# Hash attention with a gated FFN: keys' signs masked for either head on ScalarE, key operands scaled by a power of two, queries' signs spread by a transfer

## The chip, the cores and the metric

The kernel runs on one core of a Trainium2 chip. The metric is the device time in microseconds (us) of one execution. Beside it stands one execution that the hardware profiler recorded; all trace times below come from it, counted from the start of its span.

## What is computed

Four batches of eight heads, 768 positions, head dimension 64. Every query and every key gets six sign bits from a projection; a query attends only to keys whose six bits are all equal to its own. The attention output, as 3072 tokens by 512, goes through a gated FFN with 1536 hidden units.

```python
q_bits = (np.einsum('bhsd,dk->bhsk', q, proj) > 0)       # k_bits alike
mask = q_bucket[:, :, :, None] == k_bucket[:, :, None, :]
scores = np.where(mask, (1/8) * q @ k.T, -1e9)
attn = softmax(scores) @ v                                # per head
x = attn.transpose(0, 2, 1, 3).reshape(3072, 512)
out = (silu(x @ w_gate) * (x @ w_val)) @ w_out
```

## The kernel before

**Units.** Two heads form a pair, and there are 16 pairs, four to a batch (`NP` = 4). Each pair has two halves of 384 queries, and each half six key chunks (`NCH`) of 128 keys. `score(u)` (lines 451 to 464) makes one chunk's scores for both heads: float32 products of `kT` and `qT`, then bfloat16 products of the sign rows `kb` and `qb` added into the same bank (both are line 461), then an exponential on ScalarE (line 464) into `weights(u)`, called `room` or `A` in the trace. `add` (489, 493) sums the exponentials on VectorE. After six chunks `attend` (475) multiplies them with `vraw`, and ScalarE copies the result to `xT` (482).

**Signs.** `front(n)` prepares pair n. For the first five pairs (`n <= NP`, here called the early pairs) TensorE transposes q and k (378), and ScalarE copies them out (381); for later pairs VectorE transposes (423). Four products with `hash_w` (391) put the projections of two query halves and two key halves into four blocks of 32 partitions of one bank, `hps`. In each block partitions 0 to 15 belong to the first head and 16 to 31 to the second. Four ScalarE instructions take the signs (397) into the low 32 rows of `qb` and `kb`. Then `spread` writes the second set of rows, 64 to 95: for `kb` two VectorE multiplications by a column (406), one for either head, with zeros for the other head's rows; for `qb` a VectorE copy (409) in pairs 0 to 4, and a transfer on SP's queue (411) in later pairs. The columns `nudge` and `times_k` are built at the start (141 to 156). The sum of the sign products is zero for a matching key and at most minus 2**35 else, since `times_k` carries 2**34.

**The order.** The program's order is written out by hand, and each engine works through its own instructions in it. Up to pair 3 the main loop (735 to 778) does for each half: six times `score` and `add`; attention; then a number of steps of weight preparation (`prepare_on`, from `narrow`, 293 to 298, and `form`, 327, on VectorE; `scale_to`, 279 and 280, on ScalarE). In the second half of pair n the hash of pair n+1 comes after the sixth chunk, with its four signs at once, and `spread` is put on the list `rest`, which `finish(rest)` empties after the attention, ahead of the preparation. In the first half of a pair, `total(n-1)` comes after the second chunk: it sums the accumulators with products (506), takes the reciprocal on VectorE (514) and sends it over the partitions by eight transfers on SP's queue (519); `norm` then scales `xT` on VectorE (526). The bank of these sums is the same one that attention uses in the first batch.

**Loads.** `load(n+2)` stands at the end of pair n and puts q, k and v on SP's queue. q and k have one buffer each, v has two.

**Later.** From pair 4 on (`LATE`), products of the FFN (`up`, `po`, line 550) fill TensorE between the halves, and `chores`, one after each product step, hold the signs and `spread` of the next pair. The first `up` products need `xT` of the first two pairs, the second block those of pairs 2 and 3.

Of the kernel before, what the change touches and what calls it, by code (L numbers as in the profile page):

```python
# [8 lines left out]
FP32 = mybir.dt.float32  # L9
# [3 lines left out]
ALU = mybir.AluOpType  # L13
AF = mybir.ActivationFunctionType
AX = mybir.AxisListType
# [3 lines left out]
def kernel(  # L19
# [57 lines left out]
    def fetch(n, name, queue, half=None):  # L77
        b, pr = pairs[n]
        if name == "v":
            t = raws["v", n] = raw.tile([P, 2, NCH, D], FP32, tag="vraw", name="vraw")  # L80
            queue.dma_start(
                t.rearrange("p h c d -> p h (c d)"),
                v[b, 2 * pr : 2 * pr + 2].rearrange("h (p c) d -> p h (c d)", c=NCH),
            )
            return
        src = q if name == "q" else k
        if not half:
            raws[name, n] = raw.tile([P, NCH, 2, D], FP32, tag=name + "raw", name=name + "raw",
                                     bufs=1)
        t = raws[name, n]  # L90
        if n <= NP:
            cs = slice(None) if half is None else slice(half * CH, (half + 1) * CH)
            for h in range(2):
                queue.dma_start(t[:, cs, h, :],
                                src[b, 2 * pr + h].rearrange("(p c) d -> p c d", c=NCH)[:, cs, :])
            return


        blocks = t.rearrange("p c a b -> p (c a b)").rearrange(
            "p (c a d) -> p c a d", a=P // BLOCK, d=BLOCK)  # L100
        for h in range(2):
            for x in range(D // BLOCK):
                at = h * D + x * BLOCK
                queue.dma_start(
                    blocks[at : at + BLOCK],
                    src[b, 2 * pr + h][:, x * BLOCK : (x + 1) * BLOCK].rearrange(
                        "(a p c) d -> p c a d", c=NCH, p=BLOCK))

    def load(n):
        for name in "qkv":  # L110
            fetch(n, name, nc.sync)

    two_proj = konst.tile([P, NBITS], FP32, tag="proj", name="proj")
    for o in (0, D):
# [23 lines left out]


    HR = 16  # L140
    assert NBITS + 1 <= HR and 2 * HR == BLOCK
    rules = wraw.tile([P, PIECE, 2], I32, tag="words", name="rules").rearrange("p f w -> p (f w)")
    rules = rules.bitcast(FP32)[:, 0 : 3 * P].rearrange("p (x r) -> p x r", r=P)

    nc.gpsimd.memset(rules[:, 0, :], -(2.0**-120))
    nc.gpsimd.memset(rules[:, 1:3, :], 0.0)
    groups = rules.rearrange("p x (g r) -> p x g r", r=HR)
    nc.gpsimd.memset(groups[:, 0, :, NBITS : NBITS + 1], 1.0)
    for h in range(2):
        g = groups[:, 1 + h, h, :]  # L150
        nc.gpsimd.memset(g[:, 0:NBITS], OFF / 2)
        nc.gpsimd.memset(g[:, NBITS : NBITS + 1], -NBITS * OFF / 2)
    nc.vector.tensor_tensor(rules, rules, ident.unsqueeze(1).to_broadcast([P, 3, P]), op=ALU.mult)
    columns = konst.tile([P, 3], FP32, tag="columns", name="columns")
    nc.vector.tensor_reduce(out=columns, in_=rules, axis=AX.X, op=ALU.add)
    nudge, *times_k = (columns[0:BLOCK, x : x + 1] for x in range(3))

    hash_w = konst.tile([P, BLOCK], FP32, tag="hash", name="hash")
    nc.vector.memset(hash_w, 0.0)
# [210 lines left out]
    def front(n):  # L370


        def transpose(name, half):
            if (name, n) not in T:
                T[name, n] = opnd.tile([P, S], FP32, tag=name + "T", name=name + "T")
            ps = bank("tps")
            for i in range(CH):
                nc.tensor.transpose(ps[:, i * P : (i + 1) * P],
                                    raws[name, n][:, half * CH + i, :, :].rearrange("p h d -> p (h d)"),
                                    ident)  # L380
            nc.scalar.copy(T[name, n][:, half * HQ : (half + 1) * HQ], ps[:, 0:HQ])

        bits["q", n] = sides["q", n % 2]
        bits["k", n] = sides["k", n % 2]

        def hash_blocks(todo, own):


            tile_ = bank("hps")
            for i, (name, half) in enumerate(todo):  # L390
                nc.tensor.matmul(tile_[i * BLOCK : (i + 1) * BLOCK, 0:HQ], hash_w,  # L391
                                 T[name, n][:, half * HQ : (half + 1) * HQ],
                                 start=True, stop=True)
            low, high = slice(0, BLOCK), slice(D, D + BLOCK)

            def sign(i, name, half):
                nc.scalar.activation(bits[name, n][low, half * HQ : (half + 1) * HQ],
                                     tile_[i * BLOCK : (i + 1) * BLOCK, 0:HQ], AF.Sign, bias=nudge)

            def spread():  # L400
                for name in sorted({name for name, _ in todo}):
                    hs = [half for x, half in todo if x == name]
                    b = bits[name, n][:, hs[0] * HQ : (hs[-1] + 1) * HQ]
                    if name == "k":
                        for to, times in ((high, times_k[1]), (low, times_k[0])):
                            nc.vector.tensor_scalar(b[to], b[low], scalar1=times, scalar2=None,  # L406
                                                    op0=ALU.mult)
                    elif own:
                        nc.vector.tensor_copy(b[high], b[low])
                    else:  # L410
                        nc.sync.dma_start(b[high], b[low])

            return [lambda i=i, at=at: sign(i, *at) for i, at in enumerate(todo)] + [spread]

        def hash_at_once(todo):
            *signs, spread = hash_blocks(todo, True)
            for f in signs:
                f()
            return [spread]

        def transpose_blocks(name):
            T[name, n] = opnd.tile([P, S], FP32, tag=name + "T", name=name + "T")
            nc.vector.transpose(T[name, n], raws[name, n].rearrange("p c h d -> p (c h d)"))

        order = [("q", 0), ("q", 1), ("k", 0), ("k", 1)]
        if n > NP:

            return ([lambda name=name: transpose_blocks(name) for name in "qk"]
                    + [lambda: hash_blocks(order, False)])
        turns = [lambda x=x: transpose(*x) for x in order]  # L430
        if n == 0:
            return [turns[2], turns[0], lambda: hash_at_once([("k", 0)]),
                    lambda: hash_at_once([("q", 0)]), turns[3], turns[1],
                    lambda: hash_at_once([("k", 1), ("q", 1)])]
        return turns[2:] + turns[:2] + [lambda: hash_at_once(order)]


    units = [(n, half, c) for n in range(len(pairs)) for half in range(2) for c in range(NCH)]
# [9 lines left out]
    def weights(u):  # L448
        return ((early_ring if u < MOVE else late_ring) + ring)[u % NCH]

    def score(u):
        n, half, c = units[u]
        qs = slice(half * HQ, (half + 1) * HQ)
        ks = slice(c * P, (c + 1) * P)
        sc = [bank("sc")[:, 0:HQ] for _ in range(2)]
        for x, start in ((T, True), (bits, False)):
            if u < 2 and not start:
                prepare_pair(1)
            for h in range(2):
                rows = slice(h * D, (h + 1) * D)  # L460
                nc.tensor.matmul(sc[h], x["k", n][rows, ks], x["q", n][rows, qs],  # L461
                                 start=start, stop=not start)
        for h in range(2):
            nc.scalar.activation(weights(u)[:, h, 0:HQ], sc[h], AF.Exp, scale=SCALE)  # L464

    def attend(u):
        n, half, c = units[u]
# [259 lines left out]
    def finish(todo):  # L727
        while todo:
            todo.pop(0)()
# [5 lines left out]
    for u in range(0, N, NCH):  # L735
# [5 lines left out]
                nc.gpsimd.memset(t[:, :, HQ:AW], 1.0)  # L741
        for c in range(NCH):
            score(u + c)
            if u + c == 2 or not gating and half == 1 and c == NCH - 1:
                prepare_pair(1)
                if u == 0:
                    finish(rest)
            if c == 1 and half == 0 and 0 < n <= NP:
                total(n - 1)
            if c:  # L750
                add(u + c)
        if n <= NP:
            finish(waiting)
        if not gating and half == 0:
            steps = front(n + 1)
        if not gating and half == 0 and u > 0:
# [4 lines left out]
            attend(u + c)  # L761
        if not gating:
            scale_ahead()
        if half == 1 and n + 2 < len(pairs):
            load(n + 2)
        if not gating and half == 0:
            prepare_pair(2 if u > 0 else 4)
        finish(first)
        finish(rest)
        prepare_on(0 if u == LATE else 4)  # L770
        chores = []
        if half == 1 and n >= NP:
# [67 lines left out]
```

The softmax here doesn't subtract the row's maximum and nothing guards it: scores larger than these inputs give would overflow.

## Time and profile before

| what | value |
|---|---|
| three runs | median 1007.13 us (1006.35 to 1008.91) |
| profiled execution, its own time | 1007.6 us |
| its span | 1005.8 us |
| TensorE (PE) busy | 991.4 us, 99% |
| VectorE (DVE) busy | 577.2 us |
| ScalarE (ACT) busy | 392.3 us |
| scores `sc`, float32 and bfloat16 parts | 162.3 us and 66.2 us |
| FFN `up` products | 260.9 us and 197.4 us |
| granted TensorE clock, mean | 0.997 |

The profile gives each engine's busy time, the waits (who waited for whom, in total us, number of times and the longest), the chain of work that ended last, and a timeline of every engine. Busy shares are averages over stages with different limits; the stage of the early pairs lies between about 8 and 119 us, and the rest of the span is the late stage. A name in a row stands for a buffer, with the line of the program beside it.

### The profile page before, as it was taken

To read this page: it belongs to the slowest core of one execution; us is meant where nothing else is said; L and a number is where in the kernel's file an instruction comes from. 1 tells how busy PE (TensorE), PEld (TensorE's weight loads), DVE (VectorE), ACT (ScalarE), POOL (GpSimd) and SP (SyncE) were. 2 spreads that over 40 slices of the span, in tenths; PEclk is the share of its full clock that TensorE was granted. 3 is DMA by queue.
4 is the path that set the end of the run, shared out by engine and by line. 5 is a ranking of instruction groups with operands and counts; after the bars stand their busy time and mean duration, and the time that the engine had idled before them with its cause. 6 is when DMAs were issued, how large, how long until landed. Compare 5 with 4: busy or idle time off the path is not lost.

```text
span 1005.8 us, 12454 instructions
## 1 busy us (share of the span) xinstructions
PE 991.4 (99%) x4597; PEld 600.8 (60%) x4597; DVE 577.2 (57%) x904; ACT 392.3 (39%) x877; POOL 101.0 (10%) x195
## 2 busy tenths in 40 slices
PE   9988899999999999999999999999999999999998
PEld 4444455555566775555557776555555787555687
DVE  5888898888884615556454543545556442435431
ACT  6877456555433214334341223334443211222200
POOL 3222132231000000000000000000000000111000
PEclk9999999999999999999999999999999999999999
DMA  7776586876313032423430304242122011323001
GB/s 228 215 243 215 157 214 186 230 241 180 103 37 84 24 76 83 105 91 90 105 107 23 75 20 116 76 104 83 56 85 80 22 37 63 104 77 115 29 28 36
DMA packets 120557, 106.75 MB, mean 106 GB/s; under 512 B 89200, under 2 KB 103888, under 8 KB 120496
## 3 DMA queue, kind: packets, MB, share of 16 engines
q0 software_dynamic: 19104, 73.28, 22.8%
q1 hardware_dynamic: 100592, 32.48, 14.1%
q8 instruction: 36, 0.59, 0.2%
q10 hardware_dynamic: 800, 0.20, 0.1%
q14 instruction: 25, 0.20, 0.1%
HBM read 81.79 MB, written 17.30 MB: 99 GB/s over the span
## 4 chain that ended last, share of the span: by engine, by line
PE 89%; DVE 6%; DMA 1%; SPq 1%; issue 1%; ACT 1%; DVEq 0%; POOL 0%
PE up L550 43%; PE po L550 21%; PE sc L461 12%; PE av L475 10%; DVE acc L493 1%; SPq L519 1%; PE sum L506 1%; PE hps L391 1%; DMA words<-in_moe_w_out_dram 1%; DVE wo L514 1%; DVE room L295 1%; DVE room L327 1%; DMA wo<-wo 1%; DVE room L293 0%; PE idle L134 0%
## 5 line engine op out<-in xcount | busy, mean ns | idle before, releaser
L550 PE MATMUL up<-xT,room 128*128 128x384 f32 x768 | 260.9, 488 | 0.0
L550 PEld LDWEIGHTS up<-xT,room 128*128 128x128 f32 x768 | 144.6, 190 | 106.7 <-issue 9.8
L550 PE MATMUL up<-xc,room 128*128 128x384 f32 x576 | 197.4, 486 | 0.0
L461 PE MATMUL sc<-qT,kT 64*128 64x384 f32 x768 | 162.3, 498 | 0.5 <-DVE c L537 0.5
L550 PEld LDWEIGHTS up<-xc,room 128*128 128x128 f32 x576 | 109.4, 190 | 76.3
L493 DVE TENSOR_TENSOR acc<-acc,A 128x768 f32<-128x768 f32 x128 | 122.7, 958 | 15.4 <-ACT A L464 1.8
L309 POOL DMA_DIRECT2D room<-ram x96 | 51.9, 541 | 714.7 <-PE up L550 707.6
L554 DVE TENSOR_TENSOR c<-c,up 128x384 f32<-128x384 f32 x72 | 39.9, 554 | 138.3 <-PE up L550 137.9
L464 ACT ACTIVATE A<-sc 128x384 f32<-128x384 f32 x256 | 105.4, 504 | 7.5 <-PE sc L461 7.5
L461 PEld LDWEIGHTS sc<-qT,kT 64*128 64x128 f32 x768 | 68.7, 189 | 53.8 <-issue 46.8
L685 ACT COPY o<-po 128x256 f32<-128x256 f32 x48 | 17.9, 372 | 200.5 <-PE po L550 200.5
L475 PE MATMUL av<-A,vraw 128*64 128x384 f32 (+1 forms) x512 | 88.2, 486 | 0.0
L536 ACT ACTIVATE th<-c 128x384 f32<-128x384 f32 x72 | 37.6, 523 | 127.5 <-DVE c L537 88.8
L461 PE MATMUL sc<-qb,kb 64*128 64x384 bf16 x384 | 66.2, 325 | 8.4 <-DVE kb L406 8.4
L554 DVE TENSOR_TENSOR o<-o,po 128x256 f32<-128x256 f32 x36 | 15.2, 421 | 99.0 <-PE po L550 70.0
L464 ACT ACTIVATE room<-sc 128x384 f32<-128x384 f32 x128 | 54.2, 496 | 40.8 <-PE sc L461 40.8
L550 PE MATMUL po<-wo,hid 128*128 128x256 f32 x288 | 66.9, 382 | 0.0
L550 PE MATMUL po<-wo,room 128*128 128x256 f32 x288 | 66.3, 379 | 0.1
L550 PE MATMUL po<-room,hid 128*128 128x256 f32 x288 | 66.1, 379 | 0.0
L475 PEld LDWEIGHTS av<-A,vraw 128*64 128x64 f32 x512 | 36.7, 137 | 46.1 <-issue 45.2
L613 ACT COPY c<-up 128x384 f32<-128x384 f32 x72 | 34.4, 478 | 69.7 <-PE up L550 69.7
L550 PEld LDWEIGHTS po<-wo,hid 128*128 128x128 f32 x288 | 54.1, 190 | 12.1 <-issue 4.9
(107 smaller groups left out, 967.8 us busy)
## 6 DMA issues: line engine op xcount, KB each, us to landing
room<-ram POOLq DMA_DIRECT2D x48, 512.0 KB, 4.7
room<-ram POOLq DMA_DIRECT2D x48, 384.0 KB, 3.9
vraw<-in_v_dram SPq DMA_DIRECT2D x16, 384.0 KB, 3.2
ram<-room POOLq DMA_DIRECT2D x12, 512.0 KB, 5.0
out_dram<-o SPq DMA_DIRECT2D x48, 128.0 KB, 1.7
room<-in_moe_w_out_dram POOLq DMA_DIRECT2D x10, 512.0 KB, 6.3
qraw<-in_q_dram SPq DMA_DIRECT2D x48, 96.0 KB, 3.2
hid<-in_moe_w_gate_dram POOLq DMA_DIRECT2D x9, 512.0 KB, 6.8
```

Of the source, the lines that this page charges most:

```text
L295: nc.vector.scalar_tensor_tensor(out=wi, in0=hi, scalar=-(1 << 31), in1=wi, op0=ALU.bitwise_and, op1=ALU.bitwise_or)
L309: nc.gpsimd.dma_start(places[k % 2][:, PARTS[go], :], ram[k % NG][:, PARTS[go], :])
L327: nc.vector.tensor_tensor(o, x, y, op=op)
L461: nc.tensor.matmul(sc[h], x["k", n][rows, ks], x["q", n][rows, qs], start=start, stop=not start)
L464: nc.scalar.activation(weights(u)[:, h, 0:HQ], sc[h], AF.Exp, scale=SCALE)
L475: nc.tensor.matmul(ps[h * D : (h + 1) * D, 0:width], raws["v", n][:, h, c, :], a[:, h, 0:width], start=c == 0, stop=c == NCH - 1)
L493: nc.vector.tensor_tensor(acc[n, half], acc[n, half], a[:, :, 0:HQ], op=ALU.add)
L536: nc.scalar.activation(th, g, AF.Tanh, scale=0.5)
L550: nc.tensor.matmul(ps, a, x, start=start and i == 0, stop=i == len(pairs_) - 1, skip_group_check=True)
L554: nc.vector.tensor_tensor(o, a, b, op=op)
L613: nc.scalar.copy(tile_of(g, spot), c)
L685: nc.scalar.copy(o, c)
```

## The change

The sign rows change for all pairs. Keys now carry a constant row for each bit that makes the sum zero on a match: rows 0 to 5 of a head's group are signs, rows 6 to 11 are constant, +1 for queries and -1 for keys. There are eight columns of constants instead of three, on 32 partitions.

For the early pairs the transposed key is copied out multiplied by 2**-34, the sign products are small whole numbers, and the exponential's scale has the factor 2**34. Pairs 1 to 4 take the key signs straight from the bank in four ScalarE instructions, one for each half and head, with a column as scale and another as bias, so that the other head's rows become zero; the two VectorE multiplications and the query copy are gone. The query rows are spread by a transfer on SP's queue. Pair 0 keeps the VectorE steps, with columns of ones and zeros.

The hash of the next early pair moves from after the sixth chunk to after the fourth; its two query signs and their transfer follow at once, and its key signs are put on `rest`, which is now emptied between the last score and the attention. For pairs 0 to 3 the loads of q and k of pair n+2 are issued at the end of the first half of pair n instead of the second; v stays. In the late pairs the transfer of the query rows and the multiplications of the key rows become two chores, in this order, instead of one.

```diff
+    def load(n, names):
+        if n < len(pairs):
+            for name in names:
+                fetch(n, name, nc.sync)
...
+    NUDGE = -(2.0**-120)
+    nc.gpsimd.memset(rules[:, 2:8, :], 0.0)
+    nc.gpsimd.memset(rules[:, 0:2, :], NUDGE)
     groups = rules.rearrange("p x (g r) -> p x g r", r=HR)
+    nc.gpsimd.memset(groups[:, 0, :, NBITS : 2 * NBITS], 1.0)
+    nc.gpsimd.memset(groups[:, 1, :, NBITS : 2 * NBITS], -1.0)
     for h in range(2):
+        nc.gpsimd.memset(groups[:, 2 + h, h, 0:NBITS], NUDGE)
+        nc.gpsimd.memset(groups[:, 2 + h, h, NBITS : 2 * NBITS], -1.0)
+        nc.gpsimd.memset(groups[:, 4 + h, h, 0 : 2 * NBITS], 1.0)
+        nc.gpsimd.memset(groups[:, 6 + h, h, 0 : 2 * NBITS], OFF / 2)
...
+    nudge = {"q": columns[0], "k": columns[1]}
+    one_head = columns[2:4]
+    mask, times_k = columns[4:6], columns[6:8]
...
-            nc.scalar.copy(T[name, n][:, half * HQ : (half + 1) * HQ], ps[:, 0:HQ])
+            nc.scalar.activation(T[name, n][:, half * HQ : (half + 1) * HQ], ps[:, 0:HQ], AF.Copy,
+                                 scale=2 / OFF if name == "k" else 1.0)
...
+            def sign(i, name, half, to=low, **how):
+                nc.scalar.activation(bits[name, n][to, half * HQ : (half + 1) * HQ],
+                                     tile_[i * BLOCK : (i + 1) * BLOCK, 0:HQ], AF.Sign,
+                                     **(how or {"bias": nudge[name]}))
+
+            return [lambda i=i, at=at, **how: sign(i, *at, **how) for i, at in enumerate(todo)]
+
+        def spread_k(times, cols=slice(0, S)):
+            b = bits["k", n][:, cols]
+            for to, by in ((high, times[1]), (low, times[0])):
+                nc.vector.tensor_scalar(b[to], b[low], scalar1=by, scalar2=None, op0=ALU.mult)
+
+        def spread_q():
+            nc.sync.dma_start(bits["q", n][high], bits["q", n][low])
+
+        def hash_own(*todo):
+            for f in hash_blocks(todo):
                 f()
+            for name, half in todo:
+                cols = slice(half * HQ, (half + 1) * HQ)
+                if name == "k":
+                    spread_k(mask, cols)
+                else:
+                    nc.vector.tensor_copy(bits["q", n][high, cols], bits["q", n][low, cols])
+
+        def hash_early(todo):
+            q0, q1, *ks = hash_blocks(todo)
+            q0()
+            q1()
+            spread_q()
+            return [lambda k=k, h=h: k(to=(low, high)[h], bias=one_head[h], scale=mask[h])
+                    for k in ks for h in range(2)]
+
+        def hash_late(todo):
+            return hash_blocks(todo) + [spread_q, lambda: spread_k(times_k)]
...
-            nc.scalar.activation(weights(u)[:, h, 0:HQ], sc[h], AF.Exp, scale=SCALE)
+            nc.scalar.activation(weights(u)[:, h, 0:HQ], sc[h], AF.Exp,
+                                 scale=SCALE * (OFF / 2 if n <= NP else 1.0))
...
-            if u + c == 2 or not gating and half == 1 and c == NCH - 1:
+            if u + c == 2 or not gating and half == 1 and c == NCH - 3:
                 prepare_pair(1)
-                if u == 0:
-                    finish(rest)
...
         if n <= NP:
             finish(waiting)
+            finish(rest)
...
-        if half == 1 and n + 2 < len(pairs):
-            load(n + 2)
-        if not gating and half == 0:
+        if half == 1:
+            load(n + 2, "qkv" if gating else "v")
+        elif not gating:
             prepare_pair(2 if u > 0 else 4)
+            load(n + 2, "qk")
         finish(first)
-        finish(rest)
```

More of the change, by code (lines that the diff above doesn't have):

```diff
@@ L107, in fetch @@
                         "(a p c) d -> p c a d", c=NCH, p=BLOCK))
-    def load(n):
-        for name in "qkv":
-            fetch(n, name, nc.sync)
+    def load(n, names):
+        if n < len(pairs):
+            for name in names:
+                fetch(n, name, nc.sync)
     two_proj = konst.tile([P, NBITS], FP32, tag="proj", name="proj")
@@ L140 @@
     HR = 16
-    assert NBITS + 1 <= HR and 2 * HR == BLOCK
+    assert 2 * NBITS <= HR and 2 * HR == BLOCK
     rules = wraw.tile([P, PIECE, 2], I32, tag="words", name="rules").rearrange("p f w -> p (f w)")
-    rules = rules.bitcast(FP32)[:, 0 : 3 * P].rearrange("p (x r) -> p x r", r=P)
-    nc.gpsimd.memset(rules[:, 0, :], -(2.0**-120))
-    nc.gpsimd.memset(rules[:, 1:3, :], 0.0)
+    rules = rules.bitcast(FP32)[0:BLOCK, 0 : 8 * BLOCK].rearrange("p (x r) -> p x r", r=BLOCK)
+    NUDGE = -(2.0**-120)
+    nc.gpsimd.memset(rules[:, 2:8, :], 0.0)
+    nc.gpsimd.memset(rules[:, 0:2, :], NUDGE)
     groups = rules.rearrange("p x (g r) -> p x g r", r=HR)
-    nc.gpsimd.memset(groups[:, 0, :, NBITS : NBITS + 1], 1.0)
+    nc.gpsimd.memset(groups[:, 0, :, NBITS : 2 * NBITS], 1.0)
+    nc.gpsimd.memset(groups[:, 1, :, NBITS : 2 * NBITS], -1.0)
     for h in range(2):
[L150 to L156, printed above, removed]
+        nc.gpsimd.memset(groups[:, 2 + h, h, 0:NBITS], NUDGE)
+        nc.gpsimd.memset(groups[:, 2 + h, h, NBITS : 2 * NBITS], -1.0)
+        nc.gpsimd.memset(groups[:, 4 + h, h, 0 : 2 * NBITS], 1.0)
+        nc.gpsimd.memset(groups[:, 6 + h, h, 0 : 2 * NBITS], OFF / 2)
+    nc.vector.tensor_tensor(rules, rules,
+                            ident[0:BLOCK, 0:BLOCK].unsqueeze(1).to_broadcast([BLOCK, 8, BLOCK]),
+                            op=ALU.mult)
+    columns = konst.tile([P, 8], FP32, tag="columns", name="columns")
+    nc.vector.tensor_reduce(out=columns[0:BLOCK], in_=rules, axis=AX.X, op=ALU.add)
+    columns = [columns[0:BLOCK, x : x + 1] for x in range(8)]
+    nudge = {"q": columns[0], "k": columns[1]}
+    one_head = columns[2:4]
+    mask, times_k = columns[4:6], columns[6:8]
     hash_w = konst.tile([P, BLOCK], FP32, tag="hash", name="hash")
@@ L380, in transpose, with hash_blocks @@
                                     ident)
-            nc.scalar.copy(T[name, n][:, half * HQ : (half + 1) * HQ], ps[:, 0:HQ])
+            nc.scalar.activation(T[name, n][:, half * HQ : (half + 1) * HQ], ps[:, 0:HQ], AF.Copy,
+                                 scale=2 / OFF if name == "k" else 1.0)
         bits["q", n] = sides["q", n % 2]
         bits["k", n] = sides["k", n % 2]
-        def hash_blocks(todo, own):
+        low, high = slice(0, BLOCK), slice(D, D + BLOCK)
+        def hash_blocks(todo):
             tile_ = bank("hps")
@@ L393, in hash_blocks @@
                                  start=True, stop=True)
[L394 to L417, printed above, removed]
-                f()
-            return [spread]
+            def sign(i, name, half, to=low, **how):
+                nc.scalar.activation(bits[name, n][to, half * HQ : (half + 1) * HQ],
+                                     tile_[i * BLOCK : (i + 1) * BLOCK, 0:HQ], AF.Sign,
+                                     **(how or {"bias": nudge[name]}))
@@ L428, in front @@
             return ([lambda name=name: transpose_blocks(name) for name in "qk"]
-                    + [lambda: hash_blocks(order, False)])
+                    + [lambda: hash_late(order)])
         turns = [lambda x=x: transpose(*x) for x in order]
         if n == 0:
[L432 to L435, printed above, removed]
+            return [turns[2], turns[0], lambda: hash_own(("k", 0)), lambda: hash_own(("q", 0)),
+                    turns[3], turns[1], lambda: hash_own(("k", 1), ("q", 1))]
+        return turns[2:] + turns[:2] + [lambda: hash_early(order)]
     units = [(n, half, c) for n in range(len(pairs)) for half in range(2) for c in range(NCH)]
```

## The prediction

> **What bounds the kernel now.** I read the engines' shares first, then who made TensorE wait, then the stretches where it waited. The page has TensorE almost full:
>
> ```profile
> PE 991.4 (99%) x4597; PEld 600.8 (60%) x4597; DVE 577.2 (57%) x904; ACT 392.3 (39%) x877; POOL 101.0 (10%) x195
> ```
>
> So only 14.4 us (1005.8 - 991.4) of the 1005.8 are to be had by filling gaps. The waits of TensorE's own queue (us in total, times, longest) say where most of them lie:
>
> ```profile
> PE sc L461 <- DVE kb L406: 8.4, 4, 2.7
> PE av L475 <- DVE wo L514: 0.7, 2, 0.4
> PE sc L461 <- DVE c L537: 0.5, 1, 0.5
> ```
>
> The first row is the sign products at the start of a pair, waiting for VectorE's key multiplication. By the timeline the three long ones are at pairs 2, 3 and 4 (2.64, 2.49 and 2.75 us, ending at 57.04, 83.11 and 108.26), 7.9 together. The second row is attention waiting for the reciprocal, whose bank it shares. Here are three stretches of one pair each (us, then busy of PE, PEld, DVE, ACT, POOL, clock, DMA share, GB/s):
>
> ```profile
> 31.20:57.30 26.10, 23.08 (x157) 10.58 (x154) 22.82 (x31) 20.32 (x47) 8.79 (x15) 1.00 0.73 220
> 57.30:83.40 26.10, 23.61 (x149) 10.77 (x148) 22.55 (x30) 18.81 (x43) 6.19 (x10) 0.93 0.72 233
> 83.40:108.50 25.10, 21.99 (x149) 10.23 (x148) 22.16 (x29) 17.60 (x41) 5.68 (x9) 1.00 0.83 258
> ```
>
> VectorE is busy as long as TensorE in these. Its timeline shows that it sets the period (start, us, then the row; the bracket is idle time before it):
>
> ```profile
> 76.88 0.95 DVE L489 SCALAR_TENSOR_TENSOR acc<-room 128x768 f32<-128x768 f32 x1
> 77.93 4.15 DVE L493 TENSOR_TENSOR acc<-acc,A 128x768 f32<-128x768 f32 x4
> 82.11 0.85 DVE L406 TENSOR_SCALAR kb<-kb,columns 32x768 bf16<-32x768 bf16 x2
> 83.00 0.35 DVE L409 COPY qb<-qb 32x768 bf16<-32x768 bf16 x1
> ...
> 87.30 2.55 DVE L514 RECIPROCAL wo<-sum 128x384 f32<-128x384 f32 x1
> 89.77 0.90 DVE L489 SCALAR_TENSOR_TENSOR acc<-room 128x768 f32<-128x768 f32 x1
> 90.77 4.15 DVE L493 TENSOR_TENSOR acc<-acc,A 128x768 f32<-128x768 f32 x4
> 96.64 1.02 DVE L526 SCALAR_TENSOR_TENSOR xT<-xT,e,wo 128x768 f32<-128x768 f32 x1 [1.73 <-DMA wo<-wo]
> ```
>
> From the sums at 76.88 to those of the next pair at 102.02 are 25.1 us: sums 5.2, signs 1.27, seven preparation steps 3.9, reciprocal 2.5, its eight transfers to landing 6.9 (with the other half's sums inside), normalization 0.9, seven steps 4.4. No term waits for TensorE. The wait on `kb` is thus a sign that TensorE has run ahead of VectorE.
>
> After 119 us the only wait of TensorE is the 0.5 us above; a gain made before then should stay.
>
> **What the Trainium skill says.** "ScalarE: Activation LUTs", section "What ACT_TABLE_LOAD costs": with immediate scale and bias an instruction takes 186 ns + 0.833 per element, and each per-partition pointer operand adds about 93. For 384 elements that is 506 and 599; the trace has 504 (exponentials) and 570 to 575 (signs, one pointer), so a pointer is worth about 71 here. No row has two. "TensorE: Matmul & The Clock Gate", Part 1: after an idle window of about 3.4 us, which runs freely, the clock halves until a busy one has passed. The trace has the granted clock at 0.50 near 58.4 to 61.6 and 109.6 to 113, behind idle times of 2.64 and 2.75 us, and none behind 2.49. "DMA: Bandwidth & Descriptors", "Queues, rings and completion order": one engine's descriptors are consumed in ring order; so a small transfer behind loads waits for them. The trace fits: the query-sign transfers of the late pairs land after 1.9 us (median), 6.7 at worst.
>
> **The change, part by part.**
>
> *Start.* Five more fills on POOL (12 for 7), at the 0.04 to 0.10 us of the present ones; the two VectorE steps on the columns handle 256 elements for 384. The columns are ready at 4.85 and first used at 7.78: nothing, as long as those 2.9 us hold.
>
> *VectorE, pairs 1 to 4.* Each loses 0.85 + 0.35 us and the gaps, 1.27 (82.11 to 83.38): four times, 5.1 us off the chain that sets the stage.
>
> *ScalarE.* Two signs (1.17 us) now stand between exponentials eight and nine of a half, and four key signs replace two. I price one of these at 646 ns (575 + 71), between 575 (a second pointer costs nothing) and 668 (575 + 93, by the skill). Such signs run without overlap (two took 1.17), so four take 2.6 (2.3 to 2.7), 1.4 more than two (1.1 to 1.5). The 20 copies with a scale cost 504 instead of 492: 0.05 us a pair. ScalarE idles 6 to 7 us in each stretch above, but not always where it is needed. At pair 1: exponentials end at 28.15 now, at 29.3 then; key signs at 31.9 instead of 30.19. Behind them are the scaling passes (279, 280), whose result VectorE wants. It finishes its sums at 30.33, needs two steps of an older piece (1.4), and stands at 31.75 before a piece scaled only at 32.5: 0.8, with the next pass 0.2 more. So the first relief shrinks from 1.27 to about **0.3** (0 to 1.27). Later pieces are well ahead: the one scaled at 51.97 to 53.2 is taken at 59.71, and becomes ready at about 55.2.
>
> *Key signs for TensorE.* For pair 2: exponentials end at 51.3, key signs at 53.9; TensorE reaches the sign products at 54.4 (float32 part at 53.48). The 2.64 us wait is gone. Next in line: the bank of sums needs the `xT` copy, which stands behind the scaling and ends at about 55.6, and the accumulators, at about 55.7 (56.0 less 0.3). TensorE is there at 55.7: even. Attention then waits for the reciprocal.
>
> *Query signs.* Signs end at 49.7, the transfer (0.53 to issue) lands at 51.6 by the median, 56.4 by the worst; wanted at 54.4. A delay up to 55.7 moves nothing, since the reciprocal is later. On SP's queue stand ahead of it: the eight transfers of the sums, done at 44.2, and the q and k loads at 44.27 to 46.95. These start when the transposes free the buffer, now as then, so issuing them earlier in the program costs nothing; it only keeps them from queuing behind the transfer. Behind it is v, which waits for attention (53.62) anyway. For pair 4 the loads are eight small ones, until 100.8 (about 97 then); the transfer comes at about 97.5, is wanted at about 102, and the accumulators allow until 104.
>
> *Hash products* (0.65 us) only change places with two chunks of scores. *Late pairs:* the same instructions, the key multiplication one product step later, 1.3 us; no late wait on `kb` exists, so nothing.
>
> *Sum.* VectorE's chain: 0.3 + 3 × 1.27, and 0.17 because the last reciprocal need not wait for the sums' products: 4.3 us. The reciprocal of pair 3 ends at 109.45 instead of 113.75, its transfers take 6.95, `xT` is normal at 117.45 instead of 121.74. The first FFN product that needs it is the sixth, which starts at 119.46 + 5 × 0.652 = 122.7 now, so there is 1.0 us of slack at present. TensorE can be there at 109.45 + 4.05 + 3.25 = 116.75, so it waits for `xT` at 117.45: **5.2 us** earlier. The two half-speed stretches go too, but TensorE then waits for VectorE instead. 1007.6 - 5.2 = 1002.4 for the profiled execution; this stood 0.5 above the median, which gives **1001.9**.
>
> **Rivals.** *TensorE gets everything:* 7.9 us of waits plus half of 2 × 3.4 at half clock, 11.3, 995.8. It needs VectorE to have reserve; the 25.1 us above leave none. *ScalarE is late every time:* VectorE waits for a scaled piece at all four pairs and saves 0.3 each, 1.4 with the 0.17; with the slack of 1.0, 2.4 us, 1004.7. For it: the piece at 31.75. Against it: the 4 us by which later pieces lead. *Slower:* the query transfer is stuck behind the loads. It decides from 7.3 us after 49.7, where the sign products start today (57.04). A q load took up to 9.9 us to land; at that, 2.6 us lost at three pairs, and a third half-speed stretch, 1.7: 9.5 us, 1016.6. Against it: 1.9 median and 6.7 worst of 11 transfers; for it, those met an emptier DMA (share 0.7 to 0.8 here, 0.1 to 0.4 late). *The change takes no effect* is excluded by the order of instructions: eight steps leave VectorE, four come to ScalarE.
>
> **How the numbers follow.** Chances: forecast 0.68 (its own range 1000.6 to 1003.8: relief at pair 1 between 0 and 1.27, and an us for unseen waits), TensorE gets everything 0.08, ScalarE late 0.15, slower 0.09. About 0.3%, 3 us, is what a measurement of this kernel can tell from no change. The forecast lies beyond it but for 0.05; so do TensorE's case and a third of ScalarE's: faster 0.76. Same 0.15, slower 0.09. Range 999.8 to 1005.5: it leaves out most of the first rival and the slower one.
>
> **What would show it.** Right: the wait on `kb` 406 falls to the 0.5 us of pair 0; the VectorE period near 24 us; waits of attention for 514 grow to several us; a VectorE wait for 279 or 280 near 31 us; first `up` near 114. Wrong: TensorE waiting for the `qb` transfer, for ScalarE's key signs, or a half-clock stretch left; periods still of 25 us; or `up` early and the 5 us lost again to waits after 119 us.

## The result, and the profile after

The changed kernel takes 1002.33 us (median of four runs, 1001.47 to 1002.71), beside 1007.18 us before (four runs): a ratio of 0.9948, with a 95% interval of 0.9931 to 0.9966. The forecast was 1001.9. The profiled execution took 1002.31 us, its span is 1000.3.

On the page TensorE is as full as before:

```profile
PE 990.2 (99%) x4597; PEld 599.8 (60%) x4597; DVE 570.7 (57%) x892; ACT 398.4 (40%) x885; POOL 101.5 (10%) x200
```

VectorE has twelve instructions and 6.5 us less (4 × 1.20 = 4.8 of it the sign rows; the rest was not followed), ScalarE eight and 6.1 us more. The prediction speaks of eight and four steps; in instructions they are twelve and eight, and the times in its sum were those of all. The waits of TensorE's queue (us in total, times, longest) have changed owners:

```profile
PE av L500 <- DVE wo L539: 3.0, 2, 1.7
PE idle L135 <- DVE kb L132: 1.3, 1, 1.3
PE sc L485 <- DMA qb<-qb: 1.2, 1, 1.2
PE sc L485 <- DVE kb L417: 0.5, 1, 0.5
```

The wait for multiplied keys is down to pair 0's 0.5 us. TensorE now waits for the reciprocal (line 539), which VectorE makes, and once for the query transfer. VectorE's timeline (start, us, row; the bracket is idle time before it) has the same steps as before without the signs:

```profile
75.55 0.95 DVE L514 SCALAR_TENSOR_TENSOR acc<-room 128x768 f32<-128x768 f32 x1
76.61 4.15 DVE L518 TENSOR_TENSOR acc<-acc,A 128x768 f32<-128x768 f32 x4
80.67 0.50 DVE L302 TENSOR_SCALAR room<-room 128x512 int32<-128x512 int32 x1
...
84.67 2.55 DVE L539 RECIPROCAL wo<-sum 128x384 f32<-128x384 f32 x1
...
93.74 1.02 DVE L551 SCALAR_TENSOR_TENSOR xT<-xT,e,wo 128x768 f32<-128x768 f32 x1 [1.46 <-DMA wo<-wo]
...
106.63 2.55 DVE L539 RECIPROCAL wo<-sum 128x384 f32<-128x384 f32 x1
```

The preparation steps now follow the sums at once (80.67), where 1.27 us of key and query rows stood. The sums of pairs 1, 2 and 3 start at 50.78, 75.55 and 99.11 (50.80, 76.88 and 102.02 before): periods of 24.8 and 23.6 us, instead of 26.1 and 25.1.

The first FFN product starts at 113.72 instead of 119.46. This is where the stage ended in the kernel before, VectorE's last reciprocal and then TensorE's rows:

```profile
111.19 2.56 DVE L514 RECIPROCAL wo<-sum 128x384 f32<-128x384 f32 x1 [0.17 <-PE sum L506]
```

```profile
108.26 0.61 PE L461 MATMUL sc<-qb,kb 64*128 64x384 bf16 x2 [2.75 <-DVE kb L406]
...
115.42 1.52 PE L475 MATMUL av<-room,vraw 128*64 128x386 f32 x8
...
119.46 6.72 PE L550 MATMUL up<-xT,room 128*128 128x384 f32 x20
```

In the changed kernel TensorE's rows are:

```profile
104.41 0.32 PE L485 MATMUL sc<-qb,kb 64*128 64x384 bf16 x1 [1.17 <-DMA qb<-qb]
...
109.68 1.52 PE L500 MATMUL av<-room,vraw 128*64 128x386 f32 x8
111.03 2.76 PE L500 MATMUL av<-A,vraw 128*64 128x386 f32 x16
113.72 8.01 PE L575 MATMUL up<-xT,room 128*128 128x384 f32 x24
```

Of these 5.74 us, 5.5 are left in the span; no wait after 114 us accounts for the rest.

### The profile page after: what moved, and what is told of

Read it like the earlier page. It is cut to its first block, busy times and chain, and to the rows that moved or that the text cites. A ratio compares the mean times of both kernels' runs of the same rounds, so it can differ in the third digit from the quotient of the medians.

```text
span 1000.3 us, 12465 instructions
## 1 busy us (share of the span) xinstructions
PE 990.2 (99%) x4597; PEld 599.8 (60%) x4597; DVE 570.7 (57%) x892; ACT 398.4 (40%) x885; POOL 101.5 (10%) x200
## 4 chain that ended last, share of the span: by engine, by line
PE 87%; DMA 2%; DVE 1%; SPq 1%; ACT 1%; issue 1%; POOL 0%; DVEq 0%; POOLq 0%
PE up L575 43%; PE po L575 22%; PE sc L485 12%; PE av L500 9%; PE sum L531 1%; DMA words<-in_moe_w_out_dram 1%; PE hps L403 1%; SPq L104 1%; DMA wo<-wo 1%; DMA qb<-qb 0%; DMA room<-ram 0%; DVE room L359 0%; ACT A L488 0%; DVE wo L539 0%; DVE acc L518 0%
```

## The experiments

Two theories were held against each other. V: VectorE's chain of sums, preparation, reciprocal and normalization sets the early stage; the change pays because it takes steps away from VectorE. T: it pays because TensorE no longer waits for the key signs and keeps its clock. All edits are to the changed kernel. Each comparison has its own runs of the kernel before, with medians of 1007.12 us for experiments 1 to 4, 1007.52 for 5 to 8 and 1007.64 for 9 to 12.

**1. VectorE gets its work back, with nobody waiting for it.**

```diff
+    spare = konst.tile([P, S], BF16, tag="spare", name="spare")
...
+            def refill():
+                b = bits["q", n]
+                for to, by in ((high, mask[1]), (low, mask[0])):
+                    nc.vector.tensor_scalar(spare[to], b[low], scalar1=by, scalar2=None, op0=ALU.mult)
+                nc.vector.tensor_copy(spare[high], b[low])
...
-                    for k in ks for h in range(2)]
+                    for k in ks for h in range(2)] + [refill]
```

> The changed kernel, with three VectorE instructions of the old shapes put back after the key signs of pairs 1 to 4; they write a spare tile that nobody reads. Theory V (VectorE's chain sets the early stage): periods back near 26 us. At pair 1 the refill covers 0.86 us of VectorE's wait for a scaled piece, so about 0.4 is lost there, then 3 x 1.27: +4.2, less 0.4 us of slack at the first FFN products, about 1006.1 us, although TensorE waits for no key signs. Rival T (the gain is TensorE's removed wait for the key signs and its clock): nothing is lost, 1002.3 us.

Measured: 1007.62 us (1005.27 to 1012.54 in 14 runs), ratio to before 1.0006 (0.9991 to 1.0021). The gain is gone, against T. But more went than V allows (1006.1), and the runs lie far apart. The profiled run (1009.33 us) has TensorE's waits:

```profile
PE av L507 <- DVE wo L546: 5.7, 2, 3.0
PE sc L492 <- DMA qb<-qb: 3.4, 1, 3.4
```

The second row is pair 4's query transfer, issued at 102.50 behind the eight loads; it landed 7.8 us later. So this run does not separate VectorE's part from the transfer's. Experiment 12 takes the transfer of pair 4 away.

**2. More TensorE work.**

```diff
-            for i in range(CH):
+            for i in [*range(CH)] * (2 if name == "k" and n >= 2 else 1):
```

> The changed kernel, with the six key transposes of pairs 2 to 4 done twice: 0.87 us more TensorE work in the first half of pairs 1, 2 and 3, just ahead of the attention. V: the waits of attention for the reciprocal (1.67 and 1.38 us) shrink to about 0.8 and 0.5 and nothing else moves: 1002.3 to 1002.8 us. T: 3 x 0.87 = 2.6 us slower, 1004.9 us.

Measured: 1000.76 us (1000.05 to 1001.88), ratio 0.9935 (0.9922 to 0.9948). The 2.6 us of added TensorE work cost nothing at the places where they stand. The time is 1.5 us below what V gave, too; the interval overlaps that of the changed kernel, so it is not shown that this is faster. The waits of attention shrank as expected, and the first FFN product stayed where it was (113.72):

```profile
PE av L500 <- DVE wo L539: 1.7, 2, 1.0
```

```profile
113.71 8.01 PE L575 MATMUL up<-xT,room 128*128 128x384 f32 x24
```

**3. Queries' rows back on VectorE.**

```diff
+        def copy_q():
+            nc.vector.tensor_copy(bits["q", n][high], bits["q", n][low])
...
-            spread_q()
...
-                    for k in ks for h in range(2)]
+                    for k in ks for h in range(2)] + [copy_q]
```

> The changed kernel, but the query rows of pairs 1 to 4 are again copied by VectorE (0.35 us and its gap), behind its sums; keys stay with ScalarE. V: 0.38 us for each of four pairs, less what the wait for a scaled piece covers at pair 1: +1.1 to 1.5, 1003.4 to 1003.8 us, although TensorE waits some 2 us again at pairs 2, 3 and 4 for the copy. T: those waits come back, about 6 of the 7.9 us: 1006 us or more.

Measured: 1004.52 us (1004.20 to 1005.49), ratio 0.9975 (0.9965 to 0.9984), 2.2 us over the changed kernel where V gave 1.1 to 1.5 and T about 4. TensorE's old wait is back, now for the copy:

```profile
PE sc L487 <- DVE qb L434: 4.9, 3, 2.3
```

It waits 4.9 us and loses 2.2. The reciprocal of pair 3's sums starts at 108.36 instead of 106.63, 1.7 later, and the first FFN product 1.6 later. The rest is a wait of the FFN products for pair 3's `xT`, since the reciprocal's transfers took 7.4 us to the normalization instead of 6.4:

```profile
119.38 4.78 PE L577 MATMUL up<-xT,room 128*128 128x384 f32 x14 [0.59 <-DVE xT L553]
```

**4. Keys' rows back on VectorE.**

```diff
-            return [lambda k=k, h=h: k(to=(low, high)[h], bias=one_head[h], scale=mask[h])
-                    for k in ks for h in range(2)]
+            return ks + [lambda: spread_k(mask)]
```

> The changed kernel, but pairs 1 to 4 take two key signs on ScalarE and multiply them on VectorE (0.85 us and its gap), as before; the queries stay with the transfer. V: 0.9 us for each of four pairs comes back, less 0.86 at pair 1 where VectorE no longer waits for the scaled piece: +2.7, about 1005.0 us. T: the wait for the keys is back whole, 1007 us.

Measured: 1005.94 us (1003.72 to 1010.88 in 14 runs), ratio 0.9992 (0.9978 to 1.0006); this time lies between both expectations and the interval excludes neither. The trace is clearer. In the profiled run (1005.11 us) the wait for the keys is back nearly whole,

```profile
PE sc L484 <- DVE kb L417: 7.5, 4, 3.0
```

and yet the reciprocal of pair 3's sums starts at 109.03, only 2.4 us later, where V had 2.7. Four of the 14 runs took more than 1008 us; no trace here shows why.

**5. Loads behind the query transfer.**

```diff
-            load(n + 2, "qkv" if gating else "v")
+            load(n + 2, "qkv")
...
-            load(n + 2, "qk")
```

> The changed kernel, with the loads of q and k put back at the end of a pair's second half, behind the query transfer on SP's queue. Theory V, with the transfer of pair 4 as a small loss on TensorE: that transfer now lands some 2 us after its issue near 98.5, TensorE's wait of 1.2 us for it goes, and the normalization of pair 3 then sets the first FFN products: 0 to 0.4 us faster, 1001.9 to 1002.3 us; q and k start some 5 us later and are still there when the transposes want them. Rival: the loads need their place ahead; transposes of pairs 3 and 4 wait for q or k, and the time rises by 2 us or more.

Measured: 1007.50 us (1004.27 to 1012.33 in 14 runs), ratio 1.0004 (0.9990 to 1.0019). The rival came true: with the loads behind the transfer the whole gain is gone. The profiled run (1011.94 us) lies near the upper end:

```profile
64.92 1.51 PE L387 MATMUL tps<-ident,kraw 128*128 128x128 f32 x6 [4.90 <-issue]
95.70 1.51 PE L387 MATMUL tps<-ident,kraw 128*128 128x128 f32 x6 [6.82 <-DMA kraw<-in_k_dram]
```

The k loads of pair 3 were issued at 50.9 to 52.2 instead of 44.9 to 46.3, and took 5.6 to 13.2 us to land instead of 3.9; those of the next pair took 14.0 to 14.5. TensorE's first wait, for which the trace names nobody, ends at 64.92; the last of pair 3's two k loads had landed between 64.1 and 64.8. From 51.3 to 55.0 POOL issues two reads of prepared weights, a write of them and four weight loads, and the DMA engines are then full: a mean share of 1.02 in 56 to 60 us. Issued six us later, the loads met that burst, which came at the same time (51.6 to 55.3) in the changed kernel, after its loads had landed.

**6. The refill, with the loads behind.** The edits of 1 and 5 together.

> VectorE's refill of the first experiment, with the loads of q and k behind the query transfer, so that the transfer of pair 4 is not late. V: the reciprocal of pair 3's sums starts at about 110 (106.63 + 0.4 + 2 to 3 x 1.27), with no TensorE wait for qb: 1005.5 to 1006.1 us, and the runs lie closer together than in the first experiment. If instead the late transfer made all of the loss there, the time is 1002 to 1003 us.

Measured: 1012.04 us (1007.75 to 1014.39), ratio 1.0038 (1.0026 to 1.0050). A miss: the loads spoil the comparison. In the profiled run the reciprocal of pair 3's sums started at 111.27, but the eight loads of pair 5 held SP's queue until 115.1, and the reciprocal's transfers, due at 113.7, landed only for a normalization at 122.75.

**7. Normalization behind four preparation steps.**

```diff
-            finish(waiting)
+            if gating:
+                finish(waiting)
...
         prepare_on(0 if u == LATE else 4)
+        if not gating:
+            finish(waiting)
```

> The changed kernel, with the normalization of pairs 0, 1 and 2 put behind four preparation steps instead of ahead of them, so that VectorE works while the reciprocal's transfers land. V: its idle time before the normalization (2.4 + 2.3 + 1.5, 6.1 us) goes; TensorE has only its waits to give (1.7 + 1.4 + 0.4), so about 3.4 us faster, 998.9 us, with TensorE's waits for the reciprocal near zero. If VectorE's chain does not set the stage: no change, 1002.3 us.

Measured: 1002.43 us (1001.76 to 1004.98), ratio 0.9954 (0.9942 to 0.9967): no gain over the changed kernel. The time alone would speak against V. The trace of the profiled run (1004.98 us, the longest of the five; it also has a wait of 2.1 us in the late stage) shows VectorE's idle time gone and the sums of pair 3 starting at 92.46, 6.7 us earlier than in the changed kernel, and what then took it back:

```profile
PE sc L485 <- DMA qb<-qb: 5.1, 1, 5.1
```

VectorE got ahead, and pair 4's query transfer, issued at 96.47 after the last of the eight loads, landed 6.8 us later.

**8. Normalization later, loads behind.** The edits of 7 and 5 together.

> The normalization put later, and the loads of q and k behind the query transfer. V: both gains, 3.4 us and up to 1.2 us for the wait on the transfer of pair 4, since VectorE no longer covers it: about 998 us. If the loads need their place ahead, no better than the later normalization alone.

Measured: 1006.59 us (1004.90 to 1007.88), ratio 0.9992 (0.9984 to 1.0000). That is neither V's gain nor as good as 7. TensorE waits 6.5 us for k once; the loads need their place.

**9. Normalization later, pair 4's queries copied by VectorE.** To 7 is added:

```diff
-            spread_q()
+            own = [lambda: nc.vector.tensor_copy(bits["q", n][high], bits["q", n][low])]
+            if n < NP:
+                spread_q()
+                own = []
...
-                    for k in ks for h in range(2)]
+                    for k in ks for h in range(2)] + own
```

> The later normalization, with pair 4's query rows copied by VectorE instead of sent by the transfer, which stood 5.1 us late behind the eight loads there. V, now with the late transfer as the next thing that sets the end: the reciprocal of pair 3's sums starts near 100.6 instead of 106.9, the first FFN product near 107.3 instead of 115.1; 6.4 us ahead of the changed kernel, about 996 us. If the late transfer was only where an unavoidable delay showed: 1002 us, with another wait in its place.

Measured: 996.76 us (995.44 to 998.27), ratio 0.9899 (0.9885 to 0.9913): faster than both kernels. The waits for the reciprocal and for the query rows are gone from TensorE's list; the profiled run has the reciprocal at

```profile
100.26 2.55 DVE L542 RECIPROCAL wo<-sum 128x384 f32<-128x384 f32 x1
```

and the first FFN product at 107.19, as worked out (100.6 and 107.3):

```profile
107.19 8.01 PE L578 MATMUL up<-xT,room 128*128 128x384 f32 x24
```

**10. The query transfers on ScalarE's queue.** To 7 is added:

```diff
-            nc.sync.dma_start(bits["q", n][high], bits["q", n][low])
+            queue = nc.scalar if n <= NP else nc.sync
+            queue.dma_start(bits["q", n][high], bits["q", n][low])
```

> The later normalization, with the query transfers of pairs 1 to 4 issued on ScalarE's queue instead of SP's. If the loads' issue on SP's queue is what holds the transfer of pair 4: no TensorE wait for qb, 996 to 997 us, ScalarE's issue (0.5 us each) costing a little. If it is the DMA engines, full with loads and weights, that hold it: the wait stays at 3 us or more and the time near 1000 us.

Measured: 999.76 us (998.68 to 1002.39), ratio 0.9928 (0.9915 to 0.9940), between the two cases. In the profiled run the transfer was issued at 94.72, as soon as the signs were done, on a queue with nothing ahead of it; in 7 it stood 3.6 us behind its signs (done at 92.9, issued at 96.47). It still took 7.4 us to land, and TensorE waited 2.1 us for it. The stretches 94 to 96 and 96 to 98 us have a DMA share of 1.17 and 1.10, and from 89.8 to 95.0 POOL had issued six writes of prepared weights and a weight load. So the loads on SP's queue explain the late issue, and the full engines are the likely reason for the slow landing; no run moved POOL's transfers. The issue on ScalarE probably had a price too: the signs came 1.8 us later than in 7, and the sums of pair 3 start at 93.32 instead of 92.46.

**11. Only pair 4's queries copied by VectorE.** The added edit of 9, without 7.

> The changed kernel, with only pair 4's query rows copied by VectorE. V: VectorE's chain is 0.4 us longer, TensorE's wait of 1.2 us for the transfer becomes one of about 1 us for the copy: 1002.0 to 1002.8 us, no gain. If the transfer's wait set the end: 1 us faster, 1001.2 us.

Measured: 1002.66 us (1002.15 to 1004.77), ratio 0.9955 (0.9943 to 0.9967). No gain, as V says: in the profiled run TensorE waits 1.5 us for the copy instead of 1.2 for the transfer, and the reciprocal of pair 3's sums starts at 106.57 (106.63).

**12. The refill, with pair 4's copy writing the true rows.** As 1, but pair 4 has no transfer:

```diff
-            spread_q()
+            if n < NP:
+                spread_q()
...
-                nc.vector.tensor_copy(spare[high], b[low])
+                nc.vector.tensor_copy((spare if n < NP else b)[high], b[low])
```

> VectorE's refill of the first experiment, with the copy of pair 4 writing the true query rows, so that pair 4 has no transfer that can be late. V: the reciprocal of pair 3's sums starts at 110 to 110.5, 1005.5 to 1006.2 us. T, or if the late transfer made the loss in the first experiment: 1002 to 1003 us.

Measured: 1006.71 us (1004.52 to 1008.89 in 14 runs), ratio 0.9991 (0.9983 to 0.9999). Of the gain 0.9 us is left; the time is 0.5 above V's range and 3.7 above T's. VectorE in the profiled run (1007.47 us):

```profile
87.02 2.55 DVE L547 RECIPROCAL wo<-sum 128x384 f32<-128x384 f32 x1
...
110.89 2.56 DVE L547 RECIPROCAL wo<-sum 128x384 f32<-128x384 f32 x1 [0.50 <-PE sum L539]
```

The last reciprocal starts 4.3 us later than in the changed kernel, of which the bracket's 0.5 is the wait for sums that ran at half clock:

```profile
109.00:112.00 3.00, 3.00 (x15) 0.86 (x14) 2.47 (x4) 0.87 (x2) 0.54 (x1) 0.50 0.36 80
```

(The granted clock is the third number from the end.) It followed a wait of 2.33 us on TensorE, for pair 4's copy, which stands behind the two added multiplications:

```profile
107.93 0.32 PE L493 MATMUL sc<-qb,kb 64*128 64x384 bf16 x1 [2.33 <-DVE qb L446]
...
114.79 1.52 PE L508 MATMUL av<-room,vraw 128*64 128x386 f32 x8
```

So 3.8 us of the reciprocal's delay are VectorE's, about three times 1.27 (0.4 lost at pair 1, and 0.6 won back by transfers that landed sooner, lie within it). In pairs 1 to 3 TensorE waited for none of the added work. The first FFN product starts 5.1 us later than in the changed kernel, at 118.83: attention began 1.34 us after the reciprocal's end instead of 0.50, and this 0.8, with the 0.5 above, goes with TensorE's wait and the half clock behind it.

## Why the prediction was right

**What bounds.** V holds for most of the gain: TensorE's work was free (experiment 2), VectorE's was not (12), and where TensorE's wait for sign rows came back with 4.9 us, the time rose by 2.2 (3). With VectorE's idle time taken out as well, and the transfer of pair 4 out of the way, the stage shortened by another 6.5 us (9).

T has a share, at pair 4. Of the 5.74 us, 4.56 are the earlier reciprocal. Before, it ended at 113.75 and attention started only 1.67 us later; now attention starts 0.50 us after it. This makes the other 1.2, and it is TensorE's: it came late out of its last wait for `kb`. The forecast had it, as the 1.0 us by which the sixth FFN product started later than its `xT` was ready.

**VectorE, 4 × 1.27.** The reciprocals of pairs 0 to 3 start 0.52, 1.42, 2.63 and 4.56 us earlier than before. Each of the last three has its 1.27, once pair 1's part is taken as lost (below); the rest of the 4.56 is 0.27 from transfers of pair 2's sums that landed sooner (VectorE's idle time 1.46 instead of 1.73), the 0.17 for the sums, and 0.3 in small pieces.

**Pair 1's relief of 0.3.** The wait for the scaled piece was there, with the size forecast (0.8):

```profile
32.44 0.43 DVE L302 TENSOR_SCALAR room<-room 128x512 int32<-128x512 int32 x1 [0.86 <-ACT room L288]
```

The 0.52 then vanished: the reciprocal's transfers landed no earlier, and the normalization of pair 0 started at 45.66 (45.68 before). From the reciprocal's end to the normalization it took 7.44 us instead of 6.94. This spread of landing times was not in the sum, and that pair 3's transfers gave it back (6.40 us instead of 6.97) was luck.

**ScalarE.** A key sign took 666 ns, close to the upper bound of 668; I priced 646. "ScalarE: Activation LUTs", section "What ACT_TABLE_LOAD costs", gives about 93 ns to each pointer operand, and the second one measured 91 (666 - 575). The 71 that I took from exponentials against signs was too little, by 0.08 us a pair. Four took 2.73 us:

```profile
28.98 2.73 ACT L408 ACTIVATE kb<-hps,columns 32x384 bf16<-32x384 f32 x4
```

ScalarE was not the bound: pair 2's sign products start at 54.20 (forecast 54.4) without waiting for key signs.

**Query transfers.** Here a step was wrong. Pairs 1 to 3 met no wait. For pair 4 I had it issued at 97.5 and landed before it was wanted at 102. The chain of waits (start, us, what) shows

```profile
97.36 1.72 SPq L104
...
99.59 4.77 DMA qb<-qb
104.36 0.04 issue
104.41 1.13 PE sc L485 x7
```

the last load's issue drawn out to 99.07, the transfer behind it, and a landing of 4.8 us. The allowance "until 104" nearly covered it: the wait of 1.17 us made attention start 0.5 us after the reciprocal's end. The sixth product stands at 113.72 + 3.26 = 116.98, and its `xT` was ready at 116.60, so TensorE and not the normalization set the end, by 0.4. Experiment 11 shows that VectorE's copy in its place gains nothing. But the landing varies with load (4.8, 6.8, 7.8 us), and the reserve of 2 us that I gave it is used up; experiments 1 and 7 ran out of it. The order in one ring, for which I cited "DMA: Bandwidth & Descriptors", section "Queues, rings and completion order", explains only part: on another queue the transfer took 7.4 us (10).

**Loads.** That issuing them earlier "costs nothing; it only keeps them from queuing behind the transfer" was right, and I had not seen what that is worth: 5 us (5).

**Clock.** The two half-speed stretches are gone (mean clock 1.000). For the first, "TensorE then waits for VectorE instead" fits: before, TensorE waited 2.49 us at pair 3 after it, so nothing of it could reach the end. For the second it fits only in part. From pair 4's first sign products to its attention TensorE took 7.16 us before, with 3.4 us at half clock in it, and takes 5.27 now. So most of the 1.2 us above is this stretch; no run takes the stretch away and leaves the wait.

**Sum.** 5.29 us in the profiled executions' own times, 4.85 between the medians; the forecast was 5.2.

## What to carry to other kernels

Where an engine near 100% waits for another one, look at the other's own period before the wait is priced: 7.9 us of waits were removed here and the stage got 5.7 us shorter, 4.6 because VectorE's chain did, and 1.2 because the last wait, with a half-clock stretch behind it, had outlasted that chain. Test it by adding work on each side, one at a time. And count what stands on a queue around a moved transfer, with the load on the DMA engines at that moment: after the first bound was gone, a 48 KB transfer was the next one, and a load issued six us later could cost as much as the change gained.

## What the runs showed of the hardware

A 48 KB transfer within SBUF landed after 1.9 us (median of the query transfers). Pair 4's took 4.8 us in the changed kernel, 6.8 in experiment 7, 7.8 in 1 and, on ScalarE's queue, 7.4 in 10. In all four POOL had issued seven transfers of weights in the 8 us before or during it, and the DMA share was 1.0 or more for most of the time. The share alone does not tell: in the changed kernel it was 1.08 from 46 to 48 us, and the k loads under way there, 192 KB each, landed in 3.9 us. Behind POOL's bursts, in experiment 5, such loads took up to 14.5 us.

An idle time of TensorE of 2.33 us was enough for a half-clock stretch in experiment 12, where the kernel before had kept its clock after 2.49 us; all of these are shorter than the idle window that the prediction cites.
